# Two small memsets of the further folded stage D's table, on GpSimd in place of VectorE

## The chip, the cores and the metric

The kernel runs on one core of one Trainium2 chip. The metric is the device time of one execution in microseconds (us), lower is better; times compared are medians over several runs. The engines are named as in the profile: PE is TensorE's matmul, PEld its weight load, DVE is VectorE, ACT is ScalarE, POOL is GpSimd, SP is SyncE.

## The reference

The input x is 8 batches of 3072 rows with 256 columns, in float32. A mixing step takes the real part of a two-dimensional Fourier transform of each batch, and a channel mix with two branches follows:

```
X = fft(fft(x, axis=1), axis=2).real
X_prev = X shifted by one row, zeros ahead
xk = mu_k * X + (1 - mu_k) * X_prev
xr = mu_r * X + (1 - mu_r) * X_prev
k = maximum(xk @ w_k, 0)          # 256 -> 1024
v = (k * k) @ w_v                 # 1024 -> 256
r = sigmoid(xr @ w_r)             # 256 -> 256
out = r * v
```

## The kernel before

**Tiling.** The eight batches are worked off one after the other. The rows of a batch's result are split into 6 chunks of 512, so there are 48 chunks, and a chunk is worked in 4 steps: 192 steps and a short tail. In each step `k_piece` (matmuls L825) makes a quarter of the product with w_k in a PSUM tile psW, ACT writes its relu to the tile rl (L835), and after every second step DVE squares two quarters into k2 (`square`, L845). Five steps behind, `v_tile` (L866) multiplies k2 by w_v into psV; `v_out` (L888) multiplies by r on DVE and SP stores the tile o. `r_item` makes r for a chunk (matmuls L852, sigmoid L857). There are three PSUM tiles psW and two psV, used in turn, four o tiles, and two tiles each of rl, k2 and r.

**The transform of the next batches** is woven between these steps. For batch t: `load_xh` fetches the rows from DRAM on POOL's DMA queue, `fold` (L172) folds them on DVE, stage A (`a_half`, L617) and stage D (`d_half`, L679) are matmuls with tables, `c_pairs` (L746) a third one into the tile pq. `halves` (L759) makes y of pq on DVE, `diff` (L767) takes differences of neighbouring rows into d, and `mix` (`scaled` L779, then `mixed` L790) makes the tiles x, which `k_piece` reads. x has two halves, a = 0 and a = 1, and each set of four L825 matmuls reads both in turn.

**The table of stage D.** From batch 3 on, stage D works on a further folded form with the table `w_d` (128 partitions x 2 x 64). `quarter_tables` (L549) makes it once, at step 42: one matmul with a matrix `same` (L551), four copies on ACT (`evac`, L574), and two memsets (L556) that overwrite row 64 of the table's second half with -1 and +1 in alternating columns. The copy of that half writes row 64 too, so the memsets wait for it. The first `d_half` that reads `w_d` is in an event of step 53.

**What sets the order.** `at(step, f, ...)` and `event(step, ...)` list by hand which function runs in which step; the loop at the end issues for each step: `k_piece`; the items of kind "x" (`quarter_tables` among them); `v_tile`; events; the items of kind "w" (`halves`, `diff`, `mix`, `fold`, `load_gate`, `load_xh`); `v_out`; `square`. `pin_order` then ties every instruction to its forerunner on the same engine, so each engine works in the order in which the program issues. Around the table:

- step 41: the square L845;
- step 42: `quarter_tables`, then `halves(2, 15, 27)`, then `v_out`;
- step 43: `diff` for a = 0 of batch 2, the square;
- step 44: `diff` for a = 1, `v_out`;
- step 45: `mix` for a = 0, the square;
- step 46: `load_gate` with the loads of batch 4, `mix` for a = 1, `v_out`;
- step 47: the square; step 48: the first `k_piece` of batch 2.

`load_gate` (L492) is a memset of one element on DVE and an iota on POOL that writes the same element: POOL waits there, so the loads behind it in its queue start when DVE has come that far.

Of the kernel before, what the change touches and what calls it, by code (L numbers as in the profile page):

```python
# [20 lines left out]
def _v(ap, extra_offset, free_dims):  # L21
    new_ap = [list(ap.ap[0])] + [[s, c] for (s, c) in free_dims]
    return dataclasses.replace(ap, offset=ap.offset + extra_offset, ap=new_ap)
# [16 lines left out]
def kernel(  # L40
# [10 lines left out]
    nc = tc.nc  # L51
# [26 lines left out]
    def ps_w():  # L78
        return ps_slot("W", 3, 1024)
# [26 lines left out]
    V = nc.vector  # L106
# [433 lines left out]
    w_d = const.tile([P, 2, 64], FP16)  # L540
# [8 lines left out]
    def quarter_tables():  # L549
        ps = ps_w()  # L550
        nc.tensor.matmul(out=ps[:, 0:128], lhsT=same, rhs=w_eo[:, 1], start=True, stop=True)  # L551
        for g, rows in enumerate((lo64, hi64)):
            evac(w_d[rows, 0], _v(w_eo[rows], g, [(2, 64)]), "A")
            evac(w_d[rows, 1], ps[rows, 64 * g:64 * g + 64], "A")
        for k in range(2):
            V.memset(_v(w_d[64:65], 64 + k, [(2, 32)]), 2.0 * k - 1.0)  # L556

    def eo_rest():

# [10 lines left out]
    def evac(out_ap, in_ap, eng):  # L570
        if eng == "V":
            V.tensor_copy(out=out_ap, in_=in_ap)
        else:
            nc.scalar.activation(out=out_ap, in_=in_ap, func=AF.Copy)  # L574
# [409 lines left out]
    def at(step, f, *args):  # L984
        work.setdefault((step, "x" if f in (a_item, a_sum, d_item, d_small, c_item, c_tiles, turned, minus_0, r_item, quarter_tables) else "w"),
                        []).append((f, args))
# [109 lines left out]
    at(33, d_item, 2, 3)  # L1096
    at(34, turned, 0, 13)
    at(42, quarter_tables)
    for n, c in enumerate(chunks[8:]):
        at(4 * n + 36, r_item, c)  # L1100
# [106 lines left out]
```

## Time and profile before

| | |
|---|---|
| median of 3 runs | 429.12 us (429.12 to 429.25) |
| the profiled execution | 429.43 us |
| its span | 427.7 us |
| granted TensorE clock over the span | 1.00 |
| DMA, moved in all | 42.08 MB |

The span goes from the first to the last instruction that the trace holds; the profiled execution's own time is 1.73 us above it. A row of a timeline gives start and duration in us, engine, line, operation, the tile written and the tile read, their shapes, how many instructions are merged in it, and in brackets how long the engine was idle just before and what ended that. A row of a list of waits says who waited for whom: us in total, how many times, the longest. A row of a table of stretches gives the stretch, its length, then for PE, PEld, DVE, ACT and POOL the busy time with the number of instructions, and at the end the granted clock, the busy share of the DMA engines, and GB/s. A row for one line of the kernel gives least, median and greatest duration in ns, first and last start, and shapes. Consecutive instructions of one engine can overlap in these rows by a few hundredths to some tenths of a us, since an engine starts the next one before the last result is written.

### The profile page before, as it was taken

To read this page: it belongs to the slowest core of one execution; us is meant where nothing else is said; L and a number is where in the kernel's file an instruction comes from. 1 tells how busy PE (TensorE), PEld (TensorE's weight loads), DVE (VectorE), ACT (ScalarE), POOL (GpSimd) and SP (SyncE) were. 2 spreads that over 40 slices of the span, in tenths; PEclk is the share of its full clock that TensorE was granted. 3 is DMA by queue.
4 is the path that set the end of the run, shared out by engine and by line. 5 is a ranking of instruction groups with operands and counts; after the bars stand their busy time and mean duration, and the time that the engine had idled before them with its cause. 6 is when DMAs were issued, how large, how long until landed. Compare 5 with 4: busy or idle time off the path is not lost.

```text
span 427.7 us, 9640 instructions
## 1 busy us (share of the span) xinstructions
PE 420.9 (98%) x3991; PEld 295.4 (69%) x3991; DVE 367.8 (86%) x586; ACT 328.6 (77%) x409; POOL 61.7 (14%) x97
## 2 busy tenths in 40 slices
PE   8999999999999999999999999999999999999996
PEld 3767776777667777766677677767767777766765
DVE  8899999999797999979989899988999756997453
ACT  7889897878868878687786967778686877666661
POOL 7488502000050001300041000500000000000000
PEclk9999999999999999999999999999999999999999
DMA  8779966322277224932358323762232322323233
GB/s 171 109 117 189 223 144 125 75 64 60 51 132 179 61 51 82 195 91 51 79 118 177 71 54 71 141 154 59 66 75 51 75 67 60 72 63 71 66 76 98
DMA packets 35104, 42.08 MB, mean 98 GB/s; under 512 B 4114, under 2 KB 31092, under 8 KB 35060
## 3 DMA queue, kind: packets, MB, share of 16 engines
q1 hardware_dynamic: 27488, 25.41, 24.5%
q0 software_dynamic: 7264, 15.80, 22.1%
q8 instruction: 31, 0.51, 0.5%
q10 hardware_dynamic: 308, 0.26, 0.2%
q14 instruction: 13, 0.11, 0.1%
HBM read 32.08 MB, written 25.17 MB: 134 GB/s over the span
## 4 chain that ended last, share of the span: by engine, by line
PE 94%; DVE 3%; issue 1%; POOL 0%; ACT 0%; POOLq 0%; DVEq 0%
PE psW L825 38%; PE psV L866 36%; PE psW L852 10%; PE psV L878 3%; PE psW L746 1%; PE psW L679 1%; PE psW L617 1%; PE psW L235 1%; PE psW L657 1%; PE psW L635 1%; DVE k L845 1%; PE psW L714 1%; PE psV L378 1%; DVE y L759 1%; DVE d L767 0%
## 5 line engine op out<-in xcount | busy, mean ns | idle before, releaser
L835 ACT ACTIVATE rl<-psW 128x1024 f16<-128x1024 f32 x192 | 193.8, 1032 | 82.8 <-PE psW L825 78.1
L825 PE MATMUL psW<-x,wk 128*128 128x512 f16 (+1 forms) x776 | 193.8, 377 | 1.1 <-DVE x L790 0.7
L866 PE MATMUL psV<-wv_sb,k 128*128 128x256 f16 x1424 | 184.2, 273 | 0.0
L866 PEld LDWEIGHTS <-k 128*128 128x128 f16 x1424 | 136.5, 98 | 38.4
L845 DVE TENSOR_TENSOR k<-rl 128x2048 f16<-128x2048 f16 (+1 forms) x100 | 115.6, 1156 | 33.4 <-ACT rl L835 33.0
L825 PEld LDWEIGHTS <-wk 128*128 128x128 f16 x776 | 75.3, 98 | 56.0 <-issue 1.7
L888 DVE SCALAR_TENSOR_TENSOR o<-psV,r 128x512 f32<-128x512 f32 (+1 forms) x97 | 65.7, 680 | 12.1 <-PE psV L866 11.4
L790 DVE TENSOR_TENSOR x<-y,t 128x1536 f16<-128x1536 f16 (+3 forms) x74 | 62.1, 846 | 2.1
L857 ACT ACTIVATE r<-psW 128x1024 f16<-128x1024 f32 x48 | 49.5, 1032 | 0.8 <-PE psW L852 0.8
L852 PE MATMUL psW<-wr,x 128*128 128x256 f16 x384 | 49.8, 273 | 0.0
L852 PEld LDWEIGHTS <-x 128*128 128x128 f16 x384 | 37.5, 98 | 14.3
L494 POOL IOTA gate<- 1x1 int32 x7 | 2.3, 323 | 202.9 <-DVE gate L493 202.8
L574 ACT ACTIVATE g_all<-psW 128x512 f16<-128x512 f32 (+8 forms) x62 | 28.9, 542 | 1.3 <-PE psW L679 1.0
L574 ACT ACTIVATE a<-psW 128x832 f16<-128x832 f32 x31 | 25.7, 866 | 1.4 <-PE psW L617 1.4
L172 DVE TENSOR_TENSOR p<-xp,xm 112x2304 f16<-112x2304 f16 (+6 forms) x19 | 21.7, 1140 | 0.5 <-DMA xm<-in_x_dram,idx 0.5
L779 DVE TENSOR_SCALAR t<-d,muf_t 128x1536 f16<-128x1536 f16 (+3 forms) x42 | 21.9, 533 | 0.1
L574 ACT ACTIVATE pq<-psW 128x1024 f16<-128x1024 f32 (+1 forms) x24 | 20.8, 922 | 1.4 <-PE psW L746 1.4
L141 POOL DMA_INDIRECT xm<-in_x_dram,idx_g x18 | 20.2, 1121 | 5.5 <-issue 5.5
L779 DVE TENSOR_SCALAR t<-d,mu_m 128x1536 f16<-128x1536 f16 x32 | 19.8, 617 | 0.0
L767 DVE TENSOR_TENSOR d<-y 128x1664 f16<-128x1664 f16 (+5 forms) x19 | 16.7, 880 | 0.3 <-ACT y L574 0.3
L759 DVE TENSOR_TENSOR y<-pq 128x960 f16<-128x960 f16 (+1 forms) x24 | 13.5, 605 | 1.6 <-ACT pq L574 1.3
L878 PE MATMUL psV<-wv_sb,k 128*128 128x256 f16 x112 | 14.7, 273 | 0.0
(149 smaller groups left out, 226.5 us busy)
## 6 DMA issues: line engine op xcount, KB each, us to landing
out_dram<-o SPq DMA_DIRECT2D x189, 128.0 KB, 2.4
xp<-in_x_dram POOLq DMA_DIRECT2D x12, 216.0 KB, 4.4
xp<-in_x_dram POOLq DMA_DIRECT2D x13, 192.0 KB, 7.7
xp<-in_x_dram POOLq DMA_DIRECT2D x2, 384.0 KB, 7.2
wv_sb<-in_moe_w_v_dram POOLq DMA_DIRECT2D x1, 512.0 KB, 8.6
xp<-in_x_dram SPq DMA_DIRECT2D x1, 480.0 KB, 4.3
xp<-in_x_dram POOLq DMA_DIRECT2D x1, 432.0 KB, 4.9
xm<-in_x_dram,idx_g POOLq DMA_INDIRECT x18, 8.2
```

The costliest lines, as they stand in the source:

```text
L172: V.tensor_tensor(out=p[:, q0:q0 + n], in0=xp[:, q0:q0 + n], in1=_v(xm, o + 256, [(-256, n), (-1, 256)]), op=ALU.add)
L574: nc.scalar.activation(out=out_ap, in_=in_ap, func=AF.Copy)
L779: V.tensor_scalar(out=dst, in0=src, scalar1=mu, scalar2=None, op0=ALU.mult)
L790: V.tensor_tensor(out=_v(x_t[b, j, m], o, [(64 * step, hi - lo), (step, 64)]), in0=y_t[b][:, lo + 3 * m:hi + 3 * m, a], in1=x_t["t", a][:, ...
L825: nc.tensor.matmul(out=st["k", ds][:, 512 * hs + lo:512 * hs + hi], lhsT=wk_sb[m][a][:, 128 * fc:128 * fc + 128], rhs=xk[:, a, 512 * i + l ...
L835: nc.scalar.activation(out=st["rl"][:, 2 * ds:2 * ds + 2], in_=st["k", ds].rearrange("p (f t) -> p f t", f=2), func=AF.Relu, bias=0.0, sca ...
L845: V.tensor_tensor(out=k2_t[c][:, lo:hi], in0=r, in1=r, op=ALU.mult)
L852: nc.tensor.matmul(out=ps[:, 256 * tb:256 * tb + 256], lhsT=x_t[b, 1, m][:, a, 512 * i + 128 * tb: 512 * i + 128 * tb + 128], rhs=wr_sb[m] ...
L857: nc.scalar.activation(out=st["r", c], in_=ps, func=AF.Sigmoid)
L866: nc.tensor.matmul(out=st["v", tb - h][:, 256 * h:256 * h + 256], lhsT=k2_t[c][:, fc, 128 * tb:128 * tb + 128], rhs=wv_sb[:, fc], start=(f ...
L878: nc.tensor.matmul(out=st["v", tb - h][:, 256 * h:256 * h + 256], lhsT=k2_t[c][:, fc, 128 * tb:128 * tb + 128], rhs=wv_sb[:, fc], start=fc ...
L888: V.scalar_tensor_tensor(out=o.rearrange("p a b -> p (a b)")[:, 0:256 * n], in0=st["v", t0][:, 0:256 * n], scalar=16.0, in1=st["r", c][:, ...
```

## The change

The two memsets of row 64 are issued on GpSimd. What they write, where they stand in the program and what they wait for (ACT's copy of that half of the table) stay the same.

```diff
@@ -553,7 +553,7 @@
             evac(w_d[rows, 0], _v(w_eo[rows], g, [(2, 64)]), "A")
             evac(w_d[rows, 1], ps[rows, 64 * g:64 * g + 64], "A")
         for k in range(2):
-            V.memset(_v(w_d[64:65], 64 + k, [(2, 32)]), 2.0 * k - 1.0)
+            nc.gpsimd.memset(_v(w_d[64:65], 64 + k, [(2, 32)]), 2.0 * k - 1.0)
 
     def eo_rest():
```

`V` is `nc.vector`.

## The prediction

> **What bounds the kernel now.** I read the page's totals first, then PE's waits after the start, then the queue that PE waits for there, and last what that queue waits for.
>
> ```profile
> span 427.7 us, 9640 instructions
> PE 420.9 (98%) x3991; PEld 295.4 (69%) x3991; DVE 367.8 (86%) x586; ACT 328.6 (77%) x409; POOL 61.7 (14%) x97
> PE psW L825 <- DVE x L790: 0.7, 1, 0.7
> ```
>
> PE (TensorE) is busy for 98% of the span, so a change pays only if it closes a gap on PE or opens one. The third row is the one wait that the list of waits names for PE from 105 us to the end: one matmul of L825 waits for a tile x that DVE (VectorE) writes at L790. This stretch of PE's timeline holds it:
>
> ```profile
> 118.38 1.03 PE L825 MATMUL psW<-x,wk 128*128 128x512 f16 x4
> 119.24 1.04 PE L866 MATMUL psV<-wv_sb,k 128*128 128x256 f16 x8
> 120.12 0.38 PE L825 MATMUL psW<-x,wk 128*128 128x512 f16 x1
> 121.18 0.81 PE L825 MATMUL psW<-x,wk 128*128 128x512 f16 x3 [0.68 <-DVE x L790]
> 121.82 1.04 PE L852 MATMUL psW<-wr,x 128*128 128x256 f16 x8
> ```
>
> A set of four L825 matmuls takes 119.24 - 118.38 = 0.86 from its first start to the next set's, 0.215 each. The set that begins at 120.12 takes 121.82 - 120.12 = 1.70. It is the first of batch 2 (step 48): its first matmul reads half a = 0 of x, its second half a = 1, which isn't written yet. So 1.70 - 0.86 = 0.84 us is lost. Now the queue that writes x:
>
> ```profile
> 107.44 1.22 DVE L845 TENSOR_TENSOR k<-rl 128x2048 f16<-128x2048 f16 x1
> 111.57 0.12 DVE L556 MEMSET w_d<- 1x32 f16 x2 [2.91 <-ACT w_d L574]
> 111.70 1.03 DVE L759 TENSOR_TENSOR y<-pq 128x768 f16<-128x768 f16 x2
> 112.65 0.68 DVE L888 SCALAR_TENSOR_TENSOR o<-psV,r 128x512 f32<-128x512 f32 x1
> 113.25 1.01 DVE L767 TENSOR_TENSOR d<-y 128x1664 f16<-128x1664 f16 x1
> 114.18 1.22 DVE L845 TENSOR_TENSOR k<-rl 128x2048 f16<-128x2048 f16 x1
> 115.32 1.02 DVE L767 TENSOR_TENSOR d<-y 128x1664 f16<-128x1664 f16 x1
> 116.25 0.68 DVE L888 SCALAR_TENSOR_TENSOR o<-psV,r 128x512 f32<-128x512 f32 x1
> 116.85 0.61 DVE L779 TENSOR_SCALAR t<-d,muf_t 128x1536 f16<-128x1536 f16 x1
> 117.50 0.96 DVE L790 TENSOR_TENSOR x<-y,t 128x1536 f16<-128x1536 f16 x1
> 118.37 1.22 DVE L845 TENSOR_TENSOR k<-rl 128x2048 f16<-128x2048 f16 x1
> 119.52 0.62 DVE L779 TENSOR_SCALAR t<-d,muf_t 128x1536 f16<-128x1536 f16 x1
> 120.17 0.96 DVE L790 TENSOR_TENSOR x<-y,t 128x1536 f16<-128x1536 f16 x1
> 121.64 1.22 DVE L845 TENSOR_TENSOR k<-rl 128x2048 f16<-128x2048 f16 x1
> ```
>
> The two memsets that the change touches stand at the head of this run. DVE is idle for 2.91 us until ScalarE (ACT) has copied the table; then it has no idle time up to 121.13, where the x that PE waits for is done. The two instructions that cost DVE 0.12 us of work therefore hold up the whole queue that ends in PE's one late gap.
>
> **The change part by part.** It removes two instructions and one wait from DVE and puts the same on POOL (GpSimd). Three sides: what DVE does without the wait, what POOL pays, and who reads the table.
>
> DVE first. What stands next behind the memsets, and when is it ready? These rows say when its inputs are there:
>
> ```profile
> 107.58 1.51 ACT L574 ACTIVATE pq<-psW 128x1024 f16<-128x1024 f32 x2 [0.20 <-PE psW L746]
> 111.28 0.22 ACT L574 ACTIVATE w_d<-psW 64x64 f16<-64x64 f32 x1
> 111.52 1.02 ACT L835 ACTIVATE rl<-psW 128x1024 f16<-128x1024 f32 x1
> 115.31 1.02 ACT L835 ACTIVATE rl<-psW 128x1024 f16<-128x1024 f32 x1 [0.67 <-PE psW L825]
> 119.44 1.02 ACT L835 ACTIVATE rl<-psW 128x1024 f16<-128x1024 f32 x1 [0.37 <-PE psW L825]
> 107.79 1.05 PE L866 MATMUL psV<-wv_sb,k 128*128 128x256 f16 x8
> 113.37 1.04 PE L866 MATMUL psV<-wv_sb,k 128*128 128x256 f16 x8
> ```
>
> I walk the queue again with the pitches from one start to the next in the rows above, and 0.04 from an input's end to the start that waits for it. The pair of L759 (halves) needs the pq copies, done at 109.09: it starts at 109.13 in place of 111.70, 2.57 earlier. After 0.95, at 110.08, comes the L888 of step 42, whose product (PE row at 107.79) was done at 108.84; after 0.60, at 110.68, the first L767; at 111.61 the square L845 of step 43. Here a wait takes the memsets' place: its rl comes from the ACT row at 111.52 and is done at 112.54, so it starts at 112.58 in place of 114.18. The lead has shrunk from 2.57 to 1.60. After 1.14, at 113.72, the second L767; after 0.93, at 114.65, the L888 of step 44, whose product (PE row at 113.37) was done at 114.41; L779 at 115.25 and L790 at 115.90; the square of step 45 at 116.77, its rl done at 116.33; L779 at 117.92; L790 at 118.57, done at 119.53. None of these waits again, and the lead of 1.60 holds.
>
> PE wants that tile at 120.12 + 0.215 = 120.33. It is there 0.80 earlier, so the gap goes wholly: **-0.84 us**. Bounds for this term: at least the 0.68 that PE's row calls idle (the records model a matmul's end), at most the 0.96 for which the weight loads stand still:
>
> ```profile
> 121.18 0.31 PEld L825 LDWEIGHTS <-wk 128*128 128x128 f16 x2 [0.96 <-issue]
> 122.00:200.00 78.00, 78.00 (x786) 54.99 (x785) 70.93 (x98) 61.95 (x76) 9.46 (x13) 1.00 0.52 111
> 200.00:300.00 100.00, 100.00 (x1020) 70.53 (x1017) 91.47 (x128) 79.31 (x96) 11.42 (x16) 1.00 0.48 100
> 300.00:400.00 100.00, 100.00 (x887) 70.10 (x886) 81.22 (x105) 72.19 (x82) 0.00 (x0) 1.00 0.29 66
> ```
>
> I take 0.84, since it goes from start to start. It isn't given back: in the stretches from 122 to 400 (first number the length, second PE's busy time) PE is never idle at a granted clock of 1.00, and DVE and ACT have slack, so all of it moves forward by the same amount. Just behind the gap DVE could become the late one, as the square at step 47 loses some of the lead, but the rl that it needs (ACT row at 119.44) is done at 120.46, and it stood at 121.64; 1.1 is left, more than PE's 0.84.
>
> POOL next:
>
> ```profile
> 12.52 0.10 POOL L480 MEMSET m_cs<- 64x2 f16 x1
> 67.36 1.47 POOL L141 DMA_INDIRECT xm<-in_x_dram,idx_g x1 [0.30 <-issue]
> 119.69 0.47 POOL L494 IOTA gate<- 1x1 int32 x1 [50.86 <-DVE gate L493]
> 133.22 0.87 PE L679 MATMUL psW<-w_d,a 64*128 64x64 f16 x48
> ```
>
> A strided memset of this size on POOL isn't in the trace. Its cost lies between 0.10 (the two-column memset) and 0.47 (the slowest one-element instruction, the iota); I take 0.10, the same operation. The pair waits for the same ACT copy, which ends at 111.50, so it is done between 111.7 and 112.5. Nothing is queued behind it on POOL but the gate's iota and seven loads of batch 4, in program order after it, and POOL is idle for 50.86 us before that iota. The iota waits for DVE's memset of the gate, which moves forward with DVE by 1.6; so do its loads, to about 118.1, still 6 us behind the pair. The first reader of the table is d_half on PE at 133.22, some 21 us behind the pair. That cover makes the price on POOL 0. Without it each late microsecond would be one of PE.
>
> The reader, last. One of the table's writers is now POOL, so d_half waits for POOL too. The row for an instruction on PE's queue that only waits is this:
>
> ```profile
> L825 PEldq EVENT_SEMAPHORE  x1: 51/51/51, 18.2 to 18.2; - x1
> L679 PE MATMUL psW<-w_d,a x260: 190/190/200, 133.2 to 343.1; 64*128 64x64 f16 x130
> ```
>
> One such wait costs between 0 (it rides on a matmul) and 0.051; I take 0, since L679 reads tiles of other engines already and none is listed for it. The Trainium skill (Perfetto Trace Analysis, Identifying Dependency Chains) says that instructions which wait on several engines may get EventSemaphore instructions put in ahead of them. By that rule the sum would be 0.05 less of a gain, 428.33; the trace has the form, at L825, but not at L679.
>
> **The sum.** Span 427.7 - 0.84 = 426.86. The profiled execution took 429.43, 1.73 over its span, which gives 428.59; the median of the runs shown, 429.12, is 0.31 below it, so 429.12 - 0.84 = **428.28 us**. What a measurement of this kernel can tell from no change is about 0.2%, 0.86 us: the forecast is a gain that stands on that edge. With the bounds of its terms (gain 0.68 less 0.05 up to 0.96, runs apart by some 0.1) its own range is 428.05 to 428.6.
>
> **The rivals.**
>
> The wait only moves. If the square's wait at 112.58 or a following one lasts 0.8 longer than I read it, the x tile comes after 120.33 and some or all of PE's gap stays: 428.7 for half of it less some rounding, 429.1 for all. For it: DVE loses 0.97 of its 2.57 at the first such wait, and the L888 of step 44 passes by only 0.24. Against it: the ACT and PE rows that release these instructions don't depend on DVE's lead.
>
> Slower: d_half pays for every matmul. Of the 260 of L679 one in four, 65, reads the half of the table with the memset row. If each got a wait instruction of its own at 0.051, PE would lose 65 x 0.051 = 3.3 us, all on the bound, and end at 428.28 + 3.3 = 431.6. It decides from 17 such waits on (0.84 / 0.051). Against it: every L825 set reads tiles of DVE and goes into a buffer that ACT frees, and the trace lists one such instruction for that line in the whole span.
>
> Slower: the loads collide. The seven loads of batch 4 start 1.6 earlier, in among the stores of o. If a store were held until all four o tiles are taken (L888 at 112.65, 116.25, 121.04, so about 4 us each and 16 in all), psV would stay full and PE stop; a stop of 2 us gives 430.3. Median landing of a store is 2.4 us:
>
> ```profile
> out_dram<-o SPq DMA_DIRECT2D x189, 128.0 KB, 2.4
> ```
>
> so it would have to take six times as long.
>
> **How the numbers follow.** The gap closes wholly: 0.84. The wait only moves: 0.07. d_half pays: 0.06. Loads collide: 0.03. The predicted time is the first's, 428.28. Within it the bound of 0.86 us lies inside 0.68 to 0.96; I give 0.54 to a gain over it and 0.30 to one below, since the start-to-start loss misses it by 0.02 only and the weight loads' gap lies past it, while little stands between the gain and the end. So faster 0.54; same 0.30 + 0.07 = 0.37; slower 0.09. The range runs from 427.9 (the largest gain, a little less than the median's spread below it) to 428.9 (the part of the second rival in which some of the gap closes); what lies above it is the rest of that rival and both slow ones, what lies below is a gain that no row shows.
>
> **What would show it.** Right: no idle time of DVE before a w_d memset; L759 at about 109.1; DVE idle for about 0.9 before the square at 112.6; the x tile done at about 119.5; the L825 set at 120.12 takes 0.86; everything on PE behind it 0.84 earlier; two POOL memsets at about 111.6 of 0.1 to 0.47 each; the gate at about 118.1. Wrong: a PE wait for x L790 still at 121; wait instructions on PE at L679, or idle time of PE at 132; a PE gap later in the span that was not there; a POOL memset that ends after 118.

## The result and the profile after

| | before | after |
|---|---|---|
| median of 15 runs | 429.54 us (429.12 to 430.09) | 428.58 us (428.28 to 429.54) |
| ratio | | 0.9981, 95% interval 0.9973 to 0.9989 |
| span of the profiled execution | 427.7 us | 427.1 us |

The ratio isn't the quotient of the two medians, which are 0.96 us apart. By the ratio the change makes the kernel faster by 0.19% (0.11 to 0.27), 0.82 us of 429.54 (0.47 to 1.16). The profiled execution of the changed kernel started 0.3 us later into its steps than that of before (the last section shows where), so absolute times below stand 0.31 to 0.32 higher than those of before until the place of the change, and differences are taken from start to start.

DVE's queue after the change, from its timeline:

```profile
107.76 1.22 DVE L845 TENSOR_TENSOR k<-rl 128x2048 f16<-128x2048 f16 x1
109.44 1.03 DVE L759 TENSOR_TENSOR y<-pq 128x768 f16<-128x768 f16 x2 [0.46 <-ACT pq L574]
110.38 0.68 DVE L888 SCALAR_TENSOR_TENSOR o<-psV,r 128x512 f32<-128x512 f32 x1
110.98 1.01 DVE L767 TENSOR_TENSOR d<-y 128x1664 f16<-128x1664 f16 x1
112.89 1.23 DVE L845 TENSOR_TENSOR k<-rl 128x2048 f16<-128x2048 f16 x1 [0.90 <-ACT rl L835]
...
115.57 0.61 DVE L779 TENSOR_SCALAR t<-d,muf_t 128x1536 f16<-128x1536 f16 x1
116.22 0.96 DVE L790 TENSOR_TENSOR x<-y,t 128x1536 f16<-128x1536 f16 x1
117.09 1.22 DVE L845 TENSOR_TENSOR k<-rl 128x2048 f16<-128x2048 f16 x1
118.23 0.62 DVE L779 TENSOR_SCALAR t<-d,muf_t 128x1536 f16<-128x1536 f16 x1
...
118.89 0.96 DVE L790 TENSOR_TENSOR x<-y,t 128x1536 f16<-128x1536 f16 x1
```

The idle 2.91 us are gone. In their place stand 0.46 before L759, for the pq copies, and 0.90 before the next square, for its rl: DVE meets its own inputs' times and no longer the table's. The x tile is done at 118.89 + 0.96 = 119.85. PE's timeline around it:

```profile
108.10 1.05 PE L866 MATMUL psV<-wv_sb,k 128*128 128x256 f16 x8
108.99 1.03 PE L825 MATMUL psW<-x,wk 128*128 128x512 f16 x4
109.85 0.22 PE L551 MATMUL psW<-w_eo,same 128*128 128x128 f16 x1
110.22 1.02 PE L825 MATMUL psW<-x,wk 128*128 128x512 f16 x4
...
120.43 1.03 PE L825 MATMUL psW<-x,wk 128*128 128x512 f16 x4
121.30 1.04 PE L852 MATMUL psW<-wr,x 128*128 128x256 f16 x8
...
132.70 0.87 PE L679 MATMUL psW<-w_d,a 64*128 64x64 f16 x48
```

The first set of batch 2, which took 1.70 us before, takes 121.30 - 120.43 = 0.87. From the L866 at 108.10 to the first d_half matmul at 132.70 go 24.60 us; before it was 133.22 - 107.79 = 25.43. The difference, 0.83, is the gain, and it holds to the end. The last run of forty L866 matmuls, from the two timelines (before, then after):

```profile
419.02 4.66 PE L866 MATMUL psV<-wv_sb,k 128*128 128x256 f16 x40
```

```profile
418.50 4.66 PE L866 MATMUL psV<-wv_sb,k 128*128 128x256 f16 x40
```

0.52 earlier on the clock of the span, and 0.31 more with the later start: 0.83 again. POOL's timeline shows the moved pair:

```profile
111.93 0.19 POOL L556 MEMSET w_d<- 1x32 f16 x2 [42.79 <-ACT w_d L574]
118.41 0.47 POOL L494 IOTA gate<- 1x1 int32 x1 [6.28 <-DVE gate L493]
```

The wait is the same wait; POOL spends 42.79 us idle ahead of it and nothing is lost, since the next thing it has to do is the gate at 118.41.

### The profile page after: what moved, and what is told of

The parts are those of the page before. It is cut to its first block, busy times and chain, and to the rows that moved or that the text cites. A ratio compares the mean times of both kernels' runs of the same rounds, so it can differ in the third digit from the quotient of the medians.

```text
span 427.1 us, 9641 instructions
## 1 busy us (share of the span) xinstructions
PE 421.1 (99%) x3991; PEld 295.3 (69%) x3991; DVE 367.8 (86%) x584; ACT 328.6 (77%) x409; POOL 62.3 (15%) x99
## 4 chain that ended last, share of the span: by engine, by line
PE 97%; ACT 1%; DVE 1%; issue 0%; POOL 0%; POOLq 0%
PE psW L825 39%; PE psV L866 37%; PE psW L852 10%; PE psV L878 3%; PE psW L746 1%; PE psW L617 1%; PE psW L235 1%; PE psW L679 1%; PE psW L635 1%; PE psW L657 1%; PE psW L714 1%; PE psV L378 1%; ACT pq L574 0%; DVE rw L308 0%; PE psV L657 0%
## 5 line engine op out<-in xcount | busy, mean ns | idle before, releaser
L825 PE MATMUL psW<-x,wk 128*128 128x512 f16 (+1 forms) x776 | 193.6, 377 | 0.4 <-DVE x L962 0.3
L866 PE MATMUL psV<-wv_sb,k 128*128 128x256 f16 x1424 | 184.2, 273 | 0.0
L866 PEld LDWEIGHTS <-k 128*128 128x128 f16 x1424 | 136.5, 98 | 38.4
L845 DVE TENSOR_TENSOR k<-rl 128x2048 f16<-128x2048 f16 (+1 forms) x100 | 115.5, 1156 | 35.1 <-ACT rl L835 34.7
L825 PEld LDWEIGHTS <-wk 128*128 128x128 f16 x776 | 75.3, 98 | 55.1 <-issue 0.7
L779 DVE TENSOR_SCALAR t<-d,muf_t 128x1536 f16<-128x1536 f16 (+3 forms) x42 | 21.9, 532 | 0.1
L779 DVE TENSOR_SCALAR t<-d,mu_m 128x1536 f16<-128x1536 f16 x32 | 19.6, 613 | 0.0
L759 DVE TENSOR_TENSOR y<-pq 128x960 f16<-128x960 f16 (+1 forms) x24 | 13.5, 605 | 2.0 <-ACT pq L574 1.8
```

The lines of the kernel that those rows point to most:

```text
L779: V.tensor_scalar(out=dst, in0=src, scalar1=mu, scalar2=None, op0=ALU.mult)
L825: nc.tensor.matmul(out=st["k", ds][:, 512 * hs + lo:512 * hs + hi], lhsT=wk_sb[m][a][:, 128 * fc:128 * fc + 128], rhs=xk[:, a, 512 * i + l ...
L845: V.tensor_tensor(out=k2_t[c][:, lo:hi], in0=r, in1=r, op=ALU.mult)
L866: nc.tensor.matmul(out=st["v", tb - h][:, 256 * h:256 * h + 256], lhsT=k2_t[c][:, fc, 128 * tb:128 * tb + 128], rhs=wv_sb[:, fc], start=(f ...
```

## The experiments

Two questions were open. Is it the place of the wait in DVE's queue that counted, or that POOL does the work? And how much room has the queue now, that is, does PE feel DVE only past a cover (the time by which a tile is done before PE needs it)? Theory A: an instruction that waits stops everything behind it in its engine's queue, and this costs PE what the last tile of that queue comes too late, no more. The rivals are named in each expectation. All eight runs, with the stretch from that L866 of step 42 to the first d_half matmul as PE's timeline has it (start of the one, start of the other), which the later or earlier start of an execution doesn't touch. Each ratio is taken against the kernel before, run on the same chip in the same rounds. Where an edit adds lines, the rows of that run name lines two or four further on: with the memsets at step 47 L847 is the square, L890 `v_out`, L827 `k_piece` and L854 the matmuls of `r_item`; with more L779, L829 is `k_piece` and L856 those of `r_item`:

| run | L866 to d_half, us | against before | ratio of times (95%) |
|---|---|---|---|
| before | 133.22 - 107.79 = 25.43 | | |
| changed | 132.70 - 108.10 = 24.60 | -0.83 | 0.9981 (0.9973 to 0.9989) |
| memsets on DVE, step 47 | 132.87 - 108.28 = 24.59 | -0.84 | 0.9975 (0.9966 to 0.9985) |
| changed, and a wait on DVE | 133.54 - 108.09 = 25.45 | +0.02 | 1.0002 (0.9993 to 1.0011) |
| changed, one L779 more | 132.17 - 107.58 = 24.59 | -0.84 | 0.9985 (0.9976 to 0.9994) |
| changed, three L779 more | 133.38 - 107.57 = 25.81 | +0.38 | 1.0014 (1.0005 to 1.0023) |
| table at step 50, POOL | 132.40 - 108.12 = 24.28 | -1.15 | 0.9969 (0.9956 to 0.9981) |
| table at step 50, DVE | 132.37 - 108.08 = 24.29 | -1.14 | 0.9973 (0.9962 to 0.9984) |
| no memsets | 132.42 - 107.83 = 24.59 | -0.84 | 0.9981 (0.9970 to 0.9993) |
| changed, once more | 132.34 - 107.75 = 24.59 | -0.84 | 0.9981 (0.9972 to 0.9990) |

**The memsets on DVE, later in its queue.**

```diff
+    def table_row():
         for k in range(2):
             V.memset(_v(w_d[64:65], 64 + k, [(2, 32)]), 2.0 * k - 1.0)
...
     at(42, quarter_tables)
+    at(47, table_row)
```

> The two memsets stay on DVE, but stand at step 47, behind the x tile that PE waited for and ahead of the square of that step. Theory A (what counted is the wait at the head of DVE's queue at step 42): no idle time of DVE before the memsets, L759 at about 109.1 after the square, no PE gap at the first set of step 48, the same gain as with the memsets on POOL, 0.84 us or ratio 0.998, as DVE's 0.12 us lies in the 0.37 it is idle before the square of step 47. Rival B (POOL taking the work from DVE counted): no gain, ratio 1.000 and a gap of 0.84 at step 48.

DVE's timeline of this run:

```profile
119.94 0.68 DVE L890 SCALAR_TENSOR_TENSOR o<-psV,r 128x512 f32<-128x512 f32 x1
120.69 0.13 DVE L558 MEMSET w_d<- 1x32 f16 x2
120.99 1.23 DVE L847 TENSOR_TENSOR k<-rl 128x2048 f16<-128x2048 f16 x1 [0.17 <-ACT rl L837]
```

The pair runs on DVE without a wait, inside the time that DVE is idle there anyhow (0.17 of the 0.37 is left before the square). PE's first set of step 48 runs through, in 121.47 - 120.61 = 0.86, by its timeline:

```profile
120.61 1.03 PE L827 MATMUL psW<-x,wk 128*128 128x512 f16 x4
121.47 1.04 PE L854 MATMUL psW<-wr,x 128*128 128x256 f16 x8
```

The gain is whole with nothing moved to POOL. So the engine wasn't what counted; rival B falls.

**The changed kernel with a wait at the old place.**

```diff
             nc.gpsimd.memset(_v(w_d[64:65], 64 + k, [(2, 32)]), 2.0 * k - 1.0)
+        V.tensor_copy(out=probe[96:97], in_=w_d[96:97, 1, 0:32])
```

> The changed kernel (memsets on POOL) with one more DVE instruction at the old place of the memsets: a copy of 32 elements of row 96 of the table, which ACT's same copy writes, to a scratch tile. It brings back the wait for ACT alone. Theory A: DVE is idle 2.9 us there again, the x tile comes 1.6 us later, PE's gap of 0.84 is back, ratio to before 1.000 (429.1 where before is 429.1). Rival B (POOL counted): the gain stays, ratio 0.998.

DVE's timeline, then PE's (the lines stand two further on here too):

```profile
111.83 0.17 DVE L558 COPY probe<-w_d 1x32 f16<-1x32 f16 x1 [2.87 <-ACT w_d L576]
112.02 1.03 DVE L761 TENSOR_TENSOR y<-pq 128x768 f16<-128x768 f16 x2
```

```profile
120.42 0.38 PE L827 MATMUL psW<-x,wk 128*128 128x512 f16 x1
121.50 0.81 PE L827 MATMUL psW<-x,wk 128*128 128x512 f16 x3 [0.69 <-DVE x L792]
122.14 1.04 PE L854 MATMUL psW<-wr,x 128*128 128x256 f16 x8
```

An instruction of 0.17 us that does nothing for the result brings DVE's idle 2.87 us back, PE's gap with them (122.14 - 120.42 = 1.72 for the set), and the time of before. Together with the first run this shows the cause from both sides: on the same chip, the wait in that place gives 429.61 (before) and 429.82 us (this run), and its absence 428.60 with the memsets still on DVE.

**One, and three, instructions more ahead of the x tile.** In `mix`, for batch 2 and a = 0 alone, with N = 1 and N = 3:

```diff
         scaled(b, j, m, a, lo, hi)
+        if (b, j, m, a) == (2, 0, 0, 0):
+            for _ in range(N):
+                V.tensor_scalar(out=x_t["t", a][:, lo:hi], in0=x_t[b][:, lo:hi, a],
+                                scalar1=mu_f[:, a, j:j + 1], scalar2=None, op0=ALU.mult)
         mixed(b, j, m, a, lo, hi)
```

> The changed kernel with one L779 of step 45 (batch 2, a = 0) done twice: 0.65 us more in DVE's queue ahead of the x tile. The tile is done at 119.85 in the changed kernel's profile and PE's second matmul of the set stands at 120.43 + 0.215 = 120.645, 0.80 of cover. Theory A: 0.65 fits under it, no PE gap, ratio as of the changed kernel, 0.998. Rival C (PE follows DVE directly, so each delay of this queue counts in full): 0.65 us of the gain lost, ratio 0.9996.

> As the run before, with the L779 done four times: 1.95 us more ahead of the x tile. Theory A: 1.95 - 0.80 + 0.05 for the handover = 1.2 us of PE gap at the first set of step 48, so 0.84 gained and 1.2 lost, +0.36 us against before, ratio 1.0008. Rival C: 1.95 lost, +1.1 us, ratio 1.0026.

With one more (0.62 us in DVE's timeline), the x tile is written here, and PE's set follows as if nothing had happened:

```profile
119.02 0.96 DVE L790 TENSOR_TENSOR x<-y,t 128x1536 f16<-128x1536 f16 x1
```

```profile
119.91 1.03 PE L829 MATMUL psW<-x,wk 128*128 128x512 f16 x4
120.77 1.04 PE L856 MATMUL psW<-wr,x 128*128 128x256 f16 x8
```

The tile is done at 119.98 and needed at 119.91 + 0.215 = 120.125: 0.14 of the cover is left of 0.80, and the stretch is as short as the changed kernel's. (The interval of the ratio holds 0.998 and leaves rival C's 0.9996 only just outside; the trace is clearer.) With three more PE's timeline has a gap again:

```profile
119.90 0.38 PE L829 MATMUL psW<-x,wk 128*128 128x512 f16 x1
121.34 0.81 PE L829 MATMUL psW<-x,wk 128*128 128x512 f16 x3 [1.06 <-DVE x L790]
121.98 1.04 PE L856 MATMUL psW<-wr,x 128*128 128x256 f16 x8
```

The set takes 2.08 in place of 0.86, so 1.22 are lost where 1.2 was expected, and the stretch is 0.38 longer than before. Of about 1.95 us of work added to DVE, PE felt 1.22. (The interval of the ratio, 1.0005 to 1.0023, holds theory A's 1.0008 and leaves rival C's 1.0026 outside.) Rival C, which would have PE feel all of it, falls in both runs.

**The whole table at another step.** In the changed kernel (memsets on POOL) and in the kernel before (memsets on DVE):

```diff
-    at(42, quarter_tables)
+    at(50, quarter_tables)
```

> The changed kernel with the whole of quarter_tables (matmul, four ACT copies, memsets on POOL) at step 50 in place of 42. In the changed kernel's profile PE loses a second, smaller piece behind L551: the L825 set that is due at about 109.91 starts at 110.22, when ACT has freed a psW tile. At step 50 ACT is idle 0.7 us before each rl, so theory A expects that piece to go too: no gap behind L551, no gap at step 48, 0.84 + 0.31 = 1.15 us less than before, ratio 0.9973. Rival D (that piece belongs to the matmul with the matrix same and moves with it): ratio 0.998, a gap of 0.3 at step 50.

> The kernel before (memsets on DVE) with quarter_tables at step 50. DVE will wait for ACT's copies at the memsets there as well, about 1.1 us (square done at 126.7, copies at about 127.8), but its next product that PE needs, the square of step 51, has 1.1 us of cover or more (done at 130.1, read by PE from about 131.7). Theory A (a wait on DVE costs only where DVE's queue ends in a tile that PE is waiting for): the same time as the run with POOL at step 50, ratio 0.9973. Rival B (a memset on DVE costs wherever it waits): about 0.84 to 1.1 us slower than that run, ratio 0.9995 or more.

PE's timeline of the run with POOL, at step 42 and at step 50:

```profile
108.12 1.05 PE L866 MATMUL psV<-wv_sb,k 128*128 128x256 f16 x8
109.00 1.89 PE L825 MATMUL psW<-x,wk 128*128 128x512 f16 x8
110.73 1.04 PE L866 MATMUL psV<-wv_sb,k 128*128 128x256 f16 x8
...
125.30 0.22 PE L551 MATMUL psW<-w_eo,same 128*128 128x128 f16 x1
125.35 1.04 PE L866 MATMUL psV<-wv_sb,k 128*128 128x256 f16 x8
```

The two sets of L825 now run through, and L551 costs 0.05 where it stands. The gap of 0.31 didn't move with it; rival D falls. Which tile PE waited for at step 42 is worked out from the program, since the list of waits doesn't name it: L551 takes one of the three psW tiles, so the next L825 set gets the one that this copy frees, in ACT's timeline of the changed kernel:

```profile
109.29 0.87 ACT L574 ACTIVATE a<-psW 128x832 f16<-128x832 f32 x1
```

It ends at 110.16, and the set starts at 110.22. At step 50 the tile in turn is free from 124.78 on (end of ACT's rl), 1.4 us before its set starts at 126.22. DVE's timeline of the run with the memsets on DVE:

```profile
125.22 1.22 DVE L845 TENSOR_TENSOR k<-rl 128x2048 f16<-128x2048 f16 x1
127.29 0.13 DVE L556 MEMSET w_d<- 1x32 f16 x2 [0.85 <-ACT w_d L574]
127.43 0.62 DVE L779 TENSOR_SCALAR t<-d,mu_m 128x1536 f16<-128x1536 f16 x1
...
129.56 1.22 DVE L845 TENSOR_TENSOR k<-rl 128x2048 f16<-128x2048 f16 x1
```

DVE waits 0.85 us for ACT at the memsets, and it costs nothing: 24.29 against 24.28 with POOL. The square behind it starts at 129.56, 1.05 later than with POOL (128.51 there), and is done at 130.78. PE reads it in the L866 group that starts at 131.40, so at least 0.6 us of cover is left. A wait on DVE of nearly a microsecond is free here and one of 2.9 cost 0.84 eight steps earlier; what decides is the tile at the end of the queue.

These two versions are faster than before by 0.27 and 0.31%. Against the changed kernel the intervals of their ratios overlap, so the ratios alone don't tell them apart; on the same chip and in the same rounds their medians are 428.15 and 428.12 us, the changed kernel's 428.52, in line with the 0.31 that the stretch shows.

**No memsets.** In the kernel before:

```diff
-        for k in range(2):
-            V.memset(_v(w_d[64:65], 64 + k, [(2, 32)]), 2.0 * k - 1.0)
```

> The two memsets are left out altogether, so row 64 of the table's second half keeps what ACT copied and stage D of batches 3 to 7 is computed with other values. It shows what the memsets on POOL still cost. Theory A: nothing, the time of the changed kernel, ratio 0.998, PE's first matmul of L679 at the same distance from the matmul before it (0.97 us in both). Rival E (d_half pays for its wait on POOL): up to 0.05 us per wait less than the changed kernel.

> The changed kernel once more, as the measure for the three others: ratio 0.998, 0.84 us less than before.

Both stretches are 24.59 us and both ratios 0.9981: the pair on POOL and d_half's wait for it cost nothing that can be seen. Ahead of the first L679 matmul the distance is 0.97 without memsets (131.45 to 132.42) and 0.96 with them (131.38 to 132.34), so rival E's 0.05 isn't there.

## Why the prediction was right

- **The head of DVE's queue.** Predicted: L759 at 109.13, the square at 112.58 after a wait of 0.9, x done at 119.53. Measured, less the later start of 0.31: 109.13, 112.58, 119.54. The walk through the queue, pitch by pitch with each input's time, gave every start in the rows above within 0.01.
- **The gap on PE.** Predicted 0.84 from start to start; the trace gives 0.83, in the changed kernel's second profile 0.84, and the times 0.82 (0.47 to 1.16 by the interval). The start-to-start reading was the right one of the three, by the trace: the row's idle 0.68 is too small, the weight loads' 0.96 too large. The interval of the times alone would hold all three.
- **It wasn't PE's only late gap.** The prediction went by the list of waits, which names one. The same table cost PE another 0.31 behind L551, in both kernels; the forecast isn't touched by it, since the change leaves it as it is.
- **It isn't given back.** PE has no listed wait from 100 us on in the changed kernel, and the last run of matmuls comes as much earlier as the place of the change.
- **POOL.** Taken at 0.10 for each memset, between 0.10 and 0.47: the two take 0.128 each, 0.19 together, done at 112.1, 20.6 us ahead of d_half. (The upper bound was misread: a one-element iota, L275, took 0.53 early in the trace of before. Nothing rests on it.) The gate's iota came at 118.41 (118.1 plus the later start).
- **The reader.** PE got no further instruction and lost no time. The span holds 9641 instructions in place of 9640, and the one more is on POOL, of 17 ns, ahead of the memsets, while POOL was idle. The Trainium skill (Perfetto Trace Analysis, Identifying Dependency Chains) says that such an instruction may be put in ahead of one that waits on several engines; the trace agrees as far as the form goes, but doesn't show which engines this one waited for. Its row, of line 556 in the changed kernel:

```profile
L556 POOLq EVENT_SEMAPHORE  x1: 17/17/17, 111.8 to 111.8; - x1
```

- **The rivals.** The wait did move, as said, to the square's rl, and took 0.97 of the 2.57 us of lead, no more. Neither d_half's waits nor the loads, which start 1.6 us earlier, cost anything.
- **What the chances leaned on.** The forecast stood at the edge of what can be told from no change, and the chances leaned to a gain over 0.2% because the weight loads' gap reached past it. Nothing of the 0.96 beyond 0.84 was a loss; the gain is 0.19%, and its interval, 0.11 to 0.27%, lies on both sides of that edge.
- **The absolute time.** 428.28 was made from a median of 429.12 over 3 runs; over 15 runs before stood at 429.54, and 0.84 less would be 428.70. That 428.58 falls inside the narrow range of the sum (428.05 to 428.6) and not only inside the wide one (427.9 to 428.9) is luck: it comes of two medians that differ by 0.96, where the trace gives 0.83. What was right is the mechanism and the size of the gain.

## What to carry to other kernels

A tiny instruction that waits can be as dear as the queue behind it: look at the idle time ahead of cheap instructions (a memset of 0.12 us with 2.9 us of idle before it), then follow that engine's queue to the first tile that another engine is short of, input by input. The price is what that tile comes too late, past its cover, not the wait (2.9 us of wait cost 0.84; 0.85 of wait at another step cost 0). The cure is any place where the wait is met already: an idle engine, a later place in the same queue, or a later step for the whole piece, which here also took away the 0.31 that the change left.

## What the runs showed of the hardware

**Early matmuls can run at half pace, and for how long differs from execution to execution.** Eight filling matmuls (L235) come early in each execution. Their rows in PE's timelines of before, of the changed kernel and of its second run:

```profile
6.06 3.22 PE L235 MATMUL psW<-zeros 128*128 128x512 f16 x8
```

```profile
6.07 3.59 PE L235 MATMUL psW<-zeros 128*128 128x512 f16 x8
18.69 1.03 PE L825 MATMUL psW<-x,wk 128*128 128x256 f16 x8 [0.29 <-DVE x L962]
```

```profile
6.07 2.06 PE L235 MATMUL psW<-zeros 128*128 128x512 f16 x8
18.14 1.03 PE L825 MATMUL psW<-x,wk 128*128 128x256 f16 x8 [0.29 <-DVE x L962]
```

Between the ten profiles this group takes 2.06 to 3.61 us, although it starts at 6.06 to 6.08 in each; the first product of the channel mix then starts between 18.14 and 18.71. Between before and the changed kernel the group alone accounts for it: it is 0.37 longer, and the first product comes 0.37 later (18.32 and 18.69). It isn't the only source: with the memsets at step 47 the group took 3.24, 0.02 more than in before, and the first product came at 18.67. The spread of 0.57 us in that start is as large as most of the effects here, which is why the stretch from start to start separates runs that the ratios can't. The granted clock reads 1.00 in these stretches and doesn't show the half pace. The Trainium skill (TensorE: Matmul & The Clock Gate, What's actually happening) says that PE starts at half its clock and is released by a window of activity that runs freely, not from the kernel's start; starts 0.43 apart in this group (6.06, 6.49 and 6.91 in the trace of before), against 0.215 for matmuls of the same shape later, fit that. In the second run of the changed kernel only the first of the eight is slow (starts at 6.07, 6.46, 6.67 and 6.89). That the switch is the cause of the spread wasn't tried.

**An instruction on POOL takes longer beside one on DVE.** The gate's iota takes 0.12 us at 66.03 in the changed kernel, next to DVE's L845, and 0.47 at 118.41, where it ends at 118.88, just after DVE's L779 of 118.23 (ends at 118.85); in before it is 0.47 beside the L779 at 119.52 too. In all ten profiles the last four iotas start beside an L779, take 0.47 and end within 0.03 of it. The Trainium skill (SBUF — State Buffer, Who interferes with whom) has DVE and GpSimd share a pair of ports that one of them holds for a whole instruction, tensor_scalar among those that can take it; these rows agree with that, but that L779 holds the iota is argued from them, and no run tried it. The memsets at 111.93 stood beside no tensor_scalar and took 0.128 each.
